# A recurrent attention cell followed by a gated feed-forward block: the first weight pieces asked for by ScalarE, first products in column halves, and a new order of the opening

## The chip, the cores and the metric

The kernel runs on one core of a Trainium2 chip. A core has TensorE (PE), VectorE (DVE), ScalarE (ACT), GpSimd (POOL) and SyncE (SP), and 16 DMA engines that serve the queues on which SP and ACT ask for transfers. The metric is the device time of one execution in microseconds. The time before is 514.01 us, the median of three runs (513.62 to 514.46).

## The reference

Two blocks follow each other. The first is a recurrent cell over 4 batches, 8 heads, 768 steps, 40 features per head; the second is a gated feed-forward block on the 3072 resulting rows of 320 features.

```
for t in range(S):
    m_new  = maximum(f[t] + m, i[t])
    C      = exp(f[t] + m - m_new) * C + exp(i[t] - m_new) * outer(v[t], k[t])
    n      = exp(f[t] + m - m_new) * n + exp(i[t] - m_new) * k[t]
    y[t]   = sigmoid(o[t]) * (C q[t]) / maximum(abs(n . q[t]), 1)
x   = y as rows of 8 heads x 40 = 320
out = (silu(x @ w_gate) * (x @ w_val)) @ w_out        # 320 -> 1536 -> 320
```

All inputs of the cell are float32. The three weight matrices arrive as float64, 3.9 MB each.

## The kernel before, in words

**Groups.** The 768 steps are cut into 6 groups of 128 steps for all 4 batches: 512 rows a group. For each group the cell is computed in closed form (scores of q and k, weighted with exponentials of the gates, times v, plus what the state of the steps before gives), and then the feed-forward block for these rows: 12 products of 128 hidden features each with gate and value weights (`hidden`, lines 698 to 712, the tile `gv_ps` in the profile), then `project_all` with the output weights. From the second group on, the function `gated` is used, and the cell of the next groups is woven in between.

**The opening.** Group 0 has a form of its own (functions named `first_...`). There the weights of all 128 by 128 pairs of steps stand in `W0`, 32 heads of 128 x 128, in the first 8 of 13 slices of `h_sb` (line 130). The order on TensorE, written out at lines 619 to 666, is: `burn` (products of a junk tile that nothing reads), the three products that build exponents (`first_mask`, `first_inputs`, `first_maxima`), for each half of the batches the transposes of k and q (`first_turn`), the scores (`first_scores`, whose results VectorE multiplies into `W0`, line 575), the products of `W0` with v (`first_own`, one call per batch u, 8 products of a 128 x 128 stationary tile with 41 columns), then on VectorE the division (`first_x`, lines 584 to 591) and the output gate (`first_gate`), the transposes of x into `xT` (`first_seam`), and the state for the groups behind (`first_state`, `first_kept`). Then the 12 products of `hidden` begin.

**Weights.** A float64 weight is loaded as two 32-bit words and turned into a float32 on the chip. The weights come in pieces (line 159): pieces 0 and 1 hold one slice of 128 hidden features each, pieces 2 to 6 two each, pieces 7 to 9 four slices of the output weights. `piece_load` (line 161) asks for a gate part of 5 chunks of 64 rows, and the value part as 4 chunks and 1 chunk, because the chunks of the value part are turned by one place. Before, the gate part is asked for on SP's queue and the two value parts on ACT's, for pieces 0 to 4. The raw words lie in a room of the pool `conv` (two rooms in turn) or in a tile that is free at the time (`home`: slices of `h_sb`, or `wo_sb`). The turn of one slice is `scale` (two ACT instructions into `top` and `low`, lines 212 and 214), `join` (two VectorE instructions, lines 221 and 222) and `rounded` (one addition, line 229, on POOL or VectorE).

**Order of the products.** `slots` (line 970) lists what is issued behind each of the 12 products, `ahead` which slices are converted in front of which. The gates of the steps behind the first 128 (`f_sb`, `i_sb`) are summed in `late_sums`, their running maximum is taken in `late_maxima`, goes through memory (`M_dram`) and comes back spread over partitions into `w_sb` (`weights_load`), from which the exponentials of group 1 are made (`weights_sub`, `weights_mask`, `weights_exp`).

**Queues.** Each engine works through its own instructions in order. SP's and ACT's transfers wait on 8 semaphores in turn, so a transfer is asked for only when the one eight before it has landed, and ACT does nothing else while one of its transfers waits to be asked for.

The lines around the change:

```
    nc.scalar.dma_start(out=f0, in_=spread_rows(f_gate))
    nc.sync.dma_start(out=i0, in_=spread_rows(i_gate))
    nc.scalar.dma_start(out=flat(f_sb), in_=gate_rows(f_gate)[:, L:])
    nc.scalar.dma_start(out=flat(i_sb), in_=gate_rows(i_gate)[:, L:])
    ...
    for P in range(2):
        load(k_sb, k, 0, P)
        load(q_sb, q, 0, P)
        load(v_sb, v, 0, P)
    load(o_sb, o_gate, 0, 0)
```

Of the kernel before, what the change touches and what calls it, by code (L numbers as in the profile page):

```python
# [18 lines left out]
L = 128  # L19
# [5 lines left out]
def kernel(  # L25
# [47 lines left out]
    def flat(t):  # L73
        return t.rearrange("p c t -> p (c t)")
# [79 lines left out]
    nc.scalar.dma_start(out=flat(f_sb), in_=gate_rows(f_gate)[:, L:])  # L154
    nc.scalar.dma_start(out=flat(i_sb), in_=gate_rows(i_gate)[:, L:])
# [5 lines left out]
    def piece_load(p, home=None):  # L161
        kind, m, n = PIECES[p]
        if kind == "gv":
# [4 lines left out]
            queues = (nc.sync,) + 2 * (nc.scalar if p < 5 else nc.sync,)  # L168
# [4 lines left out]
        if src[0][2].dtype == F32:  # L173
            for r, cs, w in src:
# [6 lines left out]
        if home is None:  # L181
            raw = conv.tile([128, 4 * NKC * 128], U32, name="raw")
        else:
            raw = home.rearrange("p a t -> p (a t)").bitcast(U32)
        raw = raw[:, 0:2 * a * d]
        for (r, cs, w), queue in zip(src, queues):
            queue.dma_start(out=raw[r].rearrange("p (a d) -> p a d", a=a)[:, cs], in_=w.bitcast(U32))
# [48 lines left out]
    for P in range(2):  # L236
        load(k_sb, k, 0, P)
        load(q_sb, q, 0, P)
        load(v_sb, v, 0, P)
# [339 lines left out]
    def first_own(u):  # L579
        first_y[u] = bank("first_y", "gen")[:, 0:H * D1].rearrange("p (h d) -> p h d", d=D1)  # L580
        for h in range(H):
            nc.tensor.matmul(first_y[u][:, h, :], lhsT=W0[:, u * H + h, :], rhs=v_sb[:, u * H + h, :], start=True, stop=True)  # L582
# [10 lines left out]
    def first_gate(P):  # L593
        for u in (2 * P, 2 * P + 1):
            x = x_sb[:, u, 0:DM].rearrange("p (h d) -> p h d", d=D)
            nc.vector.tensor_tensor(x, x, o_sb[:, u * H:(u + 1) * H], op=ALU.mult)
# [22 lines left out]
    burn(7)  # L619
# [8 lines left out]
    first_values(0)  # L628
    first_scores(0)
    first_own(0)  # L630
    late_sums()
    first_turn(1, k_sb, kT, (A, A))
    first_x(0)
    first_turn(1, q_sb, qT, (A, V))
    load(o_sb, o_gate, 0, 1)
    piece_load(0)
    first_own(1)
    first_values(1)
    first_scores(1)
    first_x(1)  # L640
    sig(0)
    piece_load(1)
    burn(3)
    first_own(2)
    piece_load(2, h_sb[:, 1:1 + NKC])
    sig(1)
    burn(2)
    first_own(3)
    first_gate(0)
    first_x(2)  # L650
    first_x(3)
    first_gate(1)
    first_seam(0, (A, A, V))
    scale(0)
    ps1 = first_state(1, "gen")
    burn(1, "gen")
    piece_load(3, h_sb[:, NH - NKC:])
    join(0)
    first_seam(1, (A, A, V))
    rounded(0, V)  # L660
    first_kept(0, first_state(0), A)
    first_kept(1, ps1, V)
    convert(1, V)
    nc.scalar.activation(warm, warm, AF.Silu)
    piece_load(4, wo_sb)
# [28 lines left out]

    def hid(g, m):
        return h_sb[:, m, :]
# [272 lines left out]
    ahead.update({4: [6], 5: [7, 8], 6: [9], 7: [10], 8: [11], 9: [], 10: [], 11: []})  # L969
# [138 lines left out]
```

## Time and profile before

| what | value |
|---|---|
| median of three runs | 514.01 us |
| the profiled execution, its own time | 513.3 us |
| its span, first to last instruction | 511.5 us |
| TensorE busy | 505.1 us, 99% |
| VectorE, ScalarE, GpSimd busy | 332.3, 204.8, 255.0 us |
| start of the first product of `hidden` | 31.92 us |
| start of `project_all` of group 0 | 95.03 us |
| DMA over the first 90 us | 17.57 MB, mean 195 GB/s |

In the views, a line of the timeline has the start in us, the duration or busy time in us, the engine, the line of the source, the operation, the tiles written and read, the shape and the number of instructions merged; in brackets the idle time of the engine before it and what ended it. Matrix products in float32 show as two records each. PEld is the loading of stationary tiles. A DMA view gives packets and bytes of each queue (q1 is SP's, q10 ACT's), with the time that the packets took as a share of 16 engines; the sums can pass 100%, as packets overlap.

### The profile page before, as it was taken

The numbers are of one execution on the slowest core, as the hardware profiler recorded it, in microseconds if no ns is written. First come the engines' busy times: TensorE is split into PE (matmuls) and PEld (weight loads), VectorE is DVE, ScalarE is ACT, GpSimd is POOL, SyncE is SP. The second block draws the span as 40 slices with busy tenths as digits, with TensorE's granted clock in tenths as the row PEclk, the third lists the DMA queues.
The fourth block names the chain that finished last, engine by engine and source line by source line (L and its number), as shares of the span: only waits on it lengthen the run. The fifth ranks groups of instructions, "written<-read, shape, count | busy, mean of one in ns | idle before, by whom it ended". The sixth has DMA issues, their size and how long they took to land.

```text
span 511.5 us, 14788 instructions
## 1 busy us (share of the span) xinstructions
PE 505.1 (99%) x6307; PEld 428.8 (84%) x6309; DVE 332.3 (65%) x539; ACT 204.8 (40%) x394; POOL 255.0 (50%) x274
## 2 busy tenths in 40 slices
PE   8999999999999999999999999999999999999997
PEld 4964445667888899988899888899988899988896
DVE  5779767887897777687466678467658554233421
ACT  3477655448512339312339321338421340223210
POOL 1303427475879663367652457652447650166710
PEclk9999999999999999999999999999999999999999
DMA  9999999698502992501993411993101200000001
GB/s 123 174 232 238 168 194 244 148 177 119 88 1 45 143 130 39 92 3 26 156 134 42 75 21 27 156 131 43 42 3 19 37 3 27 27 1 0 1 14 38
DMA packets 205497, 43.27 MB, mean 85 GB/s; under 512 B 193432, under 2 KB 200600, under 8 KB 205432
## 3 DMA queue, kind: packets, MB, share of 16 engines
q1 hardware_dynamic: 203444, 39.49, 49.4%
q10 hardware_dynamic: 1988, 2.85, 2.4%
q8 instruction: 49, 0.80, 0.7%
q14 instruction: 16, 0.13, 0.1%
HBM read 35.68 MB, written 4.01 MB: 78 GB/s over the span
## 4 chain that ended last, share of the span: by engine, by line
PE 91%; DMA 2%; DVE 2%; issue 1%; POOL 1%; ACT 1%; SPq 0%; DVEq 0%; ACTq 0%; POOLq 0%
PE gv_x L854 26%; PE o_ps L777 23%; PE gv_y L854 21%; PE gv_ps L706 5%; PE o_ps L723 5%; DMA w_sb<-M_dram 2%; PE inter L402 2%; PE intra L411 2%; PE sp L353 2%; PE first_y L582 1%; PE add L379 1%; POOL w_sb L493 1%; PE burn L521 1%; PE tp_kq L561 1%; PE sp L571 1%
## 5 line engine op out<-in xcount | busy, mean ns | idle before, releaser
L854 PE MATMUL gv_x<-xT,wgv_sb 64*128 64x256 f32 x720 | 89.1, 377 | 0.0
L854 PEld LDWEIGHTS gv_x<-xT,wgv_sb 64*128 64x128 f32 x720 | 69.6, 187 | 7.9 <-issue 0.2
L777 PE MATMUL o_ps<-wo_sb,h_sb 128*128 128x160 f32 x480 | 67.4, 300 | 0.0
L777 PEld LDWEIGHTS o_ps<-wo_sb,h_sb 128*128 128x128 f32 x480 | 65.6, 190 | 1.7 <-issue 1.7
L902 ACT ACTIVATE h_sb<-gv_x 128x256 f32<-128x256 f32 x30 | 11.5, 383 | 117.8 <-PE gv_x L854 117.8
L706 PE MATMUL gv_ps<-xT,wgv_sb 64*128 64x512 f32 x240 | 53.7, 596 | 0.3 <-DVE wgv_sb L229 0.3
L706 PEld LDWEIGHTS gv_ps<-xT,wgv_sb 64*128 64x128 f32 x240 | 23.6, 187 | 24.4 <-issue 23.2
L854 PE MATMUL gv_y<-q_sb,wgv_sb 64*128 64x256 f32 x360 | 44.0, 377 | 0.0
L854 PE MATMUL gv_y<-xT,wgv_sb 64*128 64x256 f32 x360 | 43.9, 376 | 0.0
L854 PEld LDWEIGHTS gv_y<-q_sb,wgv_sb 64*128 64x128 f32 x360 | 34.9, 187 | 4.2 <-DVE tmp L894 0.4
L854 PEld LDWEIGHTS gv_y<-xT,wgv_sb 64*128 64x128 f32 x360 | 35.0, 187 | 3.9
L364 POOL TENSOR_TENSOR vw_sb<-v_sb,w_sb 128x656 f32<-128x656 f32 x10 | 14.6, 1467 | 41.2 <-ACT w_sb L509 40.0
L777 PE MATMUL o_ps<-wT,S 128*128 128x160 f32 x240 | 33.4, 299 | 0.0
L777 PEld LDWEIGHTS o_ps<-wT,S 128*128 128x128 f32 x240 | 32.9, 190 | 0.0
L509 ACT ACTIVATE w_sb<-w_sb,g_T 128x64 f32<-128x64 f32 x128 | 31.0, 334 | 0.0
L854 PE MATMUL gv_x<-q_sb,sw 64*128 64x256 f32 x240 | 31.0, 376 | 0.0
L875 POOL TENSOR_TENSOR h_sb<-x_sb 128x512 f32<-128x512 f32 x12 | 15.8, 1314 | 24.6 <-ACT x_sb L874 24.6
L895 POOL TENSOR_TENSOR tmp<-tmp 128x512 f32<-128x512 f32 x15 | 20.0, 1332 | 14.5 <-DVE tmp L894 14.5
L875 POOL TENSOR_TENSOR h_sb<-tmp 128x512 f32<-128x512 f32 x13 | 16.5, 1269 | 21.5 <-ACT tmp L874 21.5
L744 POOL TENSOR_TENSOR S<-h_sb 128x256 f32<-128x256 f32 x30 | 22.6, 752 | 9.2 <-DVE h_sb L875 7.3
L854 PE MATMUL gv_y<-q_sb,sw 64*128 64x256 f32 x200 | 27.0, 388 | 0.0
L723 PE MATMUL o_ps<-wo_sb,h_sb 128*128 128x320 f32 x96 | 26.9, 437 | 0.0
(221 smaller groups left out, 984.6 us busy)
## 6 DMA issues: line engine op xcount, KB each, us to landing
w_sb<-M_dram SPq DMA_DIRECT2D x10, 512.0 KB, 7.1
k_sb<-in_k_dram SPq DMA_DIRECT2D x12, 320.0 KB, 7.4
v_sb<-in_v_dram SPq DMA_DIRECT2D x12, 320.0 KB, 5.5
o_sb<-in_o_gate_dram SPq DMA_DIRECT2D x12, 320.0 KB, 6.8
raw<-in_moe_w_out_dram SPq DMA_DIRECT2D x3, 1280.0 KB, 7.5
x_sq<-k_sb SPq DMA_DIRECT2D x64, 40.0 KB, 2.0
q_sb<-in_q_dram SPq DMA_DIRECT2D x32, 64.0 KB, 3.8
out_dram<-tmp SPq DMA_DIRECT2D x24, 80.0 KB, 1.7
```

Source lines behind the costliest of these rows:

```text
L353: nc.tensor.matmul(sp[two][half(i), a, :], lhsT=kT[feats(two), P * UA + a, half(i)], rhs=qT[feats(two), P * UA + a, half(i)], start=True, ...
L364: eng.tensor_tensor(vw_sb[:, heads(P)], v_sb[:, heads(P)], w_sb[:, heads(P), last].to_broadcast([128, UH, D1]), op=ALU.mult)
L402: nc.tensor.matmul(inter[two][half(i), a, :], lhsT=qT[feats(two), P * UA + a, half(i)], rhs=state(2 * n + i)[feats(two), P * UA + a, :], s ...
L509: nc.scalar.activation(w_sb[:, h], w_sb[:, h], AF.Exp, bias=g_T[:, n, h:h + 1], scale=-1.0)
L706: nc.tensor.matmul(ps[i], lhsT=wgv_sb[half(i), m, kc, :], rhs=x[half(i), kc, :], start=(kc == 0), stop=(kc == NKC - 1))
L723: nc.tensor.matmul(ps[u], lhsT=hid(g, m)[:, ts(u, L)], rhs=wo_sb[:, m, :], start=(m == 0), stop=(m == NFC - 1))
L744: eng.tensor_tensor(S1[:, k], lo[:, second_half], hi[:, second_half], op=ALU.add)
L777: nc.tensor.matmul(node[x][:, i], lhsT=lhs(k)[:, ts(i, L)], rhs=rhs(k), start=start and k == 0 and i == 0, stop=stop and k == KH - 1, skip ...
L854: nc.tensor.matmul(ps[:, i, cols], lhsT=lhs(c)[half(i)], rhs=rhs(c)[half(i)], start=start and c == 0, stop=stop and c == n - 1, skip_group ...
L875: (nc.vector if k == KH - 1 else nc.gpsimd).tensor_tensor(h_sb[:, 2 * k + 1], uw[:, 0], uw[:, 1], op=ALU.mult)
L895: nc.gpsimd.tensor_tensor(uw[:, :, second_half], uw[:, :, second_half], uw[:, :, first_half], op=ALU.add)
L902: nc.scalar.activation(h[:, first_half], x[:, 0, first_half], AF.Silu)
```

## The change

- ACT asks for pieces 0 and 1 in the beginning, in front of its first exponentials: gate part and first value part of each. The last value chunk (64 KB) goes to SP's queue, between the loads of k, q and v. Pieces 0 and 1 share one room of `conv`. For the other pieces the last value chunk moves from ACT's queue to SP's.
- The late gates (`f_sb`, `i_sb`) are asked for on SP behind piece 2, and `late_sums` moves from the opening to behind the first product of `hidden`; `late_maxima` and `late_decay` move to the place behind the second.
- `first_own` makes each product in two halves of 64 stationary columns.
- In the opening, `scale`, `join` and `rounded` of slice 0 move to between the transposes and scores of the second half; `rounded(0)` and `rounded(1)` go to POOL, and the first `first_gate` too. Both copies of the second q transposes are on ACT. `first_state(0)` goes in front of the seams. Of the `burn` products, burn(7) at the start becomes burn(5), and burn(3), burn(2), burn(1) between the later steps are gone.
- The rooms of raw pieces change: piece 2 in `conv`, piece 3 in slices 1 to 5 of `h_sb`. So the hidden features of the first group are written to other slices (`first_slots`).
- The load of `w_sb` goes in front of piece 6, the first steps on it one product earlier; the conversion of slices 10 and 11 one product later.

```diff
-    nc.scalar.dma_start(out=flat(f_sb), in_=gate_rows(f_gate)[:, L:])
-    nc.scalar.dma_start(out=flat(i_sb), in_=gate_rows(i_gate)[:, L:])
+    def late_gates():
+        nc.sync.dma_start(out=flat(f_sb), in_=gate_rows(f_gate)[:, L:])
+        nc.sync.dma_start(out=flat(i_sb), in_=gate_rows(i_gate)[:, L:])
...
+    raw_pair, homes = [], {}
+    def first_raw():
+        if not raw_pair:
+            raw_pair.append(conv.tile([128, 4 * NKC * 128], U32, name="raw"))
+        return raw_pair[0]
-    def piece_load(p, home=None):
+    def piece_load(p, home=None, parts=(0, 1, 2)):
...
-            queues = (nc.sync,) + 2 * (nc.scalar if p < 5 else nc.sync,)
+            queues = (nc.scalar if p < 2 else nc.sync, nc.scalar if p < 5 else nc.sync, nc.sync)
...
-        if home is None:
+        if p < 2:
+            raw = first_raw()[:, p * 2 * a * d:(p + 1) * 2 * a * d]
+        elif p in homes:
+            raw = homes[p]
+        elif home is None:
...
-    for P in range(2):
-        load(k_sb, k, 0, P)
-        load(q_sb, q, 0, P)
-        load(v_sb, v, 0, P)
+    load(k_sb, k, 0, 0)
+    load(q_sb, q, 0, 0)
+    piece_load(0, parts=(0, 1))
+    load(v_sb, v, 0, 0)
+    piece_load(1, parts=(0,))
+    load(k_sb, k, 0, 1)
+    piece_load(0, parts=(2,))
+    piece_load(1, parts=(1,))
+    load(q_sb, q, 0, 1)
+    load(v_sb, v, 0, 1)
+    piece_load(1, parts=(2,))
     load(o_sb, o_gate, 0, 0)
...
         for h in range(H):
-            nc.tensor.matmul(first_y[u][:, h, :], lhsT=W0[:, u * H + h, :], rhs=v_sb[:, u * H + h, :], start=True, stop=True)
+            for i in range(2):
+                nc.tensor.matmul(first_y[u][half(i), h, :], lhsT=W0[:, u * H + h, half(i)], rhs=v_sb[:, u * H + h, :],
+                                 start=True, stop=True)
...
-    def first_gate(P):
+    def first_gate(P, eng):
...
-            nc.vector.tensor_tensor(x, x, o_sb[:, u * H:(u + 1) * H], op=ALU.mult)
+            eng.tensor_tensor(x, x, o_sb[:, u * H:(u + 1) * H], op=ALU.mult)
...
-    burn(7)
+    burn(5)
...
     first_values(0)
+    load(o_sb, o_gate, 0, 1)
     first_scores(0)
     first_own(0)
-    late_sums()
     first_turn(1, k_sb, kT, (A, A))
     first_x(0)
-    first_turn(1, q_sb, qT, (A, V))
-    load(o_sb, o_gate, 0, 1)
-    piece_load(0)
     first_own(1)
+    scale(0)
+    first_turn(1, q_sb, qT, (A, A))
+    join(0)
     first_values(1)
+    first_x(1)
+    rounded(0)
     first_scores(1)
-    first_x(1)
+    piece_load(2, parts=(1,))
     sig(0)
-    piece_load(1)
-    burn(3)
+    piece_load(2, parts=(0, 2))
+    late_gates()
+    first_gate(0, G)
     first_own(2)
-    piece_load(2, h_sb[:, 1:1 + NKC])
+    piece_load(3, h_sb[:, 1:1 + NKC], (0, 2))
+    piece_load(4, wo_sb, (0, 2))
     sig(1)
-    burn(2)
     first_own(3)
-    first_gate(0)
     first_x(2)
+    ps0 = first_state(0)
     first_x(3)
-    first_gate(1)
+    first_gate(1, V)
     first_seam(0, (A, A, V))
-    scale(0)
+    first_kept(0, ps0, A)
+    first_seam(1, (A, A, V))
+    scale(1)
     ps1 = first_state(1, "gen")
-    burn(1, "gen")
-    piece_load(3, h_sb[:, NH - NKC:])
-    join(0)
-    first_seam(1, (A, A, V))
-    rounded(0, V)
-    first_kept(0, first_state(0), A)
+    join(1)
+    rounded(1)
+    piece_load(3, h_sb[:, 1:1 + NKC], (1,))
     first_kept(1, ps1, V)
-    convert(1, V)
+    convert(2, V)
+    piece_load(4, wo_sb, (1,))
     nc.scalar.activation(warm, warm, AF.Silu)
-    piece_load(4, wo_sb)
...
+    first_slots = (8, 9, 10, 11, 12, 0, 6, 7, 1, 2, 3, 4)
     def hid(g, m):
-        return h_sb[:, m, :]
+        return h_sb[:, first_slots[m], :]
...
-    ahead.update({4: [6], 5: [7, 8], 6: [9], 7: [10], 8: [11], 9: [], 10: [], 11: []})
+    ahead.update({4: [6], 5: [7, 8], 6: [9], 7: [], 8: [10], 9: [11], 10: [], 11: []})
     slots = {
-        0: [run(convert, 2, V), run(late_maxima), run(load_all, k_sb, k, 1),
-            run(nc.sync.dma_start, out=M_dram, in_=flat(M_sb)), run(load_all, q_sb, q, 1)],
-        1: [run(piece_load, 6), run(late_decay)],
-        2: [run(nc.scalar.activation, step1, step1, AF.Exp), run(decay_rows), run(weights_load, 1), run(load_all, v_sb, v, 1)],
+        0: [run(late_sums), run(load_all, k_sb, k, 1)],
+        1: [run(late_maxima), run(nc.sync.dma_start, out=M_dram, in_=flat(M_sb)), run(load_all, q_sb, q, 1),
+            run(weights_load, 1), run(piece_load, 6), run(late_decay)],
+        2: [run(nc.scalar.activation, step1, step1, AF.Exp), run(decay_rows), run(load_all, v_sb, v, 1)],
...
-        6: [run(turn, 1, (A, A), (A, V)), run(piece_load, 7)],
-        7: [run(weights_sub, 1, 0), run(weights_mask, 0), run(weights_sub, 1, 1), run(weights_mask, 1), run(nc.gpsimd.memset, q_sb, 0.0)],
-        8: [run(weights_exp, 0), run(weights_exp, 1), run(weigh_values, G, 0), run(weigh_values, G, 1),
-            run(piece_load, 8)],
+        6: [run(turn, 1, (A, A), (A, V)), run(piece_load, 7), run(weights_sub, 1, 0), run(weights_mask, 0), run(weights_sub, 1, 1), run(weights_mask, 1)],
+        7: [run(nc.gpsimd.memset, q_sb, 0.0), run(weights_exp, 0), run(weights_exp, 1), run(weigh_values, G, 0), run(weigh_values, G, 1)],
+        8: [run(piece_load, 8)],
```

## The prediction

> **What bounds the kernel now.** I read the page's engine shares, then the chain that ended last, then the timeline of the first 36 us and of 60 to 100 us, then the DMA queues in short windows.
>
> ```profile
> PE 505.1 (99%) x6307; PEld 428.8 (84%) x6309; DVE 332.3 (65%) x539; ACT 204.8 (40%) x394; POOL 255.0 (50%) x274
> PE 91%; DMA 2%; DVE 2%; issue 1%; POOL 1%; ACT 1%; SPq 0%; DVEq 0%; ACTq 0%; POOLq 0%
> ```
>
> TensorE is the bound and has work throughout. So the change can only move the time at which the dense products begin (31.92 us), and the stalls between there and the end of the first group.
>
> ```profile
> 1.19 3.17 PE L521 MATMUL burn<-junk 128*128 128x512 bf16 x7 [1.19 <-DVE warm L246]
> 11.24 1.08 PE L561 MATMUL tp_kq<-ident,q_sb 128*128 128x128 f32 x8
> 12.52 2.06 PE L571 MATMUL sp<-qT,kT 64*128 64x128 f32 x32 [0.20 <-ACT qT L142]
> 13.79 2.48 DVE L575 TENSOR_TENSOR h_sb<-sp,h_sb 128x512 f32<-128x512 f32 x4 [0.74 <-PE sp L571]
> 18.52 1.88 PE L582 MATMUL first_y<-v_sb,h_sb 128*128 128x41 f32 x16
> 20.32 2.06 PE L571 MATMUL sp<-qT,kT 64*128 64x128 f32 x32
> 28.04 1.13 PE L604 MATMUL add<-vw_sb,k_sb 128*64 128x41 f32 x32
> 29.33 1.25 PE L616 MATMUL tp_x<-ident,x_sb 128*128 128x128 f32 x10 [0.16 <-ACT top L212]
> 30.96 0.81 DVE L229 CUSTOM_DVE_ANT_0 wgv_sb<-wgv_sb,low 128x1280 uint16<-128x1280 uint16 x1
> 31.92 4.56 PE L706 MATMUL gv_ps<-xT,wgv_sb 64*128 64x512 f32 x20 [0.28 <-DVE wgv_sb L229]
> ```
>
> The opening is one chain: q lands, is turned (11.24), scores, VectorE's multiplications, own products, again for the second half (20.32), division, gate, seam (29.33). At its end the first dense product waits for VectorE's last step on slice 0 (30.96), 0.9 us after the first seam copies would have let it go.
>
> DMA windows at 18 to 19 us, at 19.5 to 21 us (as ACT's first piece comes in) and at 23.5 to 26 us:
>
> ```profile
> q1 hardware_dynamic: 1248, 0.20, 137.8%
> ...
> q10 hardware_dynamic: 245, 0.24, 58.5%
> q1 hardware_dynamic: 367, 0.06, 24.7%
> ...
> DMA packets 542, 0.52 MB, mean 209 GB/s; under 512 B 32, under 2 KB 542, under 8 KB 542
> ```
>
> Alone, SP's queue moves 0.20 MB in 1 us of small packets; beside the piece 0.06 MB in 1.5 us. The DMA engines have no room: a piece takes its time from the loads.
>
> **The change part by part.**
>
> *Pieces 0 and 1 early.* ACT asks for 320 + 256 + 320 + 256 = 1152 KB from about 2 us on, in front of nearly all of q, v and the second k; 160 KB of late gates leave that place. Net 992 KB (1.016 MB). Price per MB: in 19.5 to 21 us, 0.24 MB cost SP's queue 1.5 x 0.153 (153 GB/s over 10 to 19 us) - 0.06 = 0.17 MB, 1.1 us; for 1.016 MB 4.7 us. At 209 GB/s (23.5 to 26) it is 4.9 us. In 20 to 21 us, 0.22 MB took 75.4% of the engines' time, so 3.5 us. Over 4.5 to 8.5 us the queues moved only 137 GB/s where 198 were seen, room for 0.25 MB, so the low end is about 2 us, the high end 4.9. I take 4.3: the first row is nearest in kind, but its start-up lull is paid once in a burst. Landing times (issue plus time to landing): first q 2.26 + 8.7 = 10.96, now 15.3; second k 7.82 + 7.4 = 15.2, now 19.5; second q, turned at 17.6 and spaced like the others, 17.5, now 22.1 with the 64 KB chunk (0.3 us) ahead of it. o's second half was behind the pieces anyway and moves from 24.6 to about 27; its sigmoid is then done by 29, before the gate at 30. The Trainium skill, "DMA: Bandwidth & Descriptors", section "Issuing engines are not separate DMA queues", says that transfers asked for by several engines share the same 16 DMA engines and that only sequencer time is saved. By that rule the whole of 209 GB/s is paid, 4.9 us, and the sum below would be 0.6 us more, 515.5; the trace at 19.5 us leans that way.
>
> *The chain with these landings.* Turn of q 15.3, scores 1.28 later (as 11.24 to 12.52) 16.6; multiplications after 1.27, the first pair (1.24) done 19.1. An own product in halves has the form of line 604 (128 x 64 stationary, 41 columns, halves in turn): 1.13 us for 32 records against 1.88 now; I take 1.13, between -0.75 and 0. Four calls save 3.0 us of TensorE, of which two (1.5 us) are on the path. Own(0) until 20.2, turn of k 21.3, own(1) 22.5, turn of q (landed 22.1) 23.6. ACT copies k until 21.9, then scale(0) (0.81 + 0.70, as at 28.45) until 23.4, and only then the first q copy (0.6), 24.0: scale is queued ahead of the copy that the scores wait for. Scores 24.1, first pair of multiplications 26.6, all 27.85; own(2) beside, own(3) until 29.0; division (four steps, 1.1) 30.1, gate (0.88) 31.0, POOL's copy 0.35, seam with its first copies 1.35 (29.33 to about 30.5, one more copy in front): **first dense product at 32.7, 0.8 later than 31.92**. Without any delay of the loads the same chain would end at 28.4; break-even is a delay of 3.5 us. join(0) on VectorE (1.31, at 22.8) lies beside the turn of q; uncovered it costs 1.3. On POOL, rounded(0) (1.55, as at 43.22) stands ahead of the first gate (two of some 0.7, half of line 553's 1.29), done at 29.5; the seam needs it at 30.2. Late_sums leave VectorE (1.47) where it was not last. The burns gone were beside waits (they took 0.33 and 0.38 of the chain); two fewer at the start bring the exponents forward by at most 0.9, covered by the landing of q.
>
> *Dense products 0 to 5.* Slice 1 is now added on POOL: copies 0.55, scale 0.81, join 1.31, addition 1.55, some 0.1 between: 4.35 us after the first product starts, which takes 4.36. Slack zero, cost 0 to 1; take 0.2. Late_sums behind product 0 put a scan (1.47) in front of join(3), and a memset and a subtraction (0.62 + 1.53) in front of rounded(3) on POOL: it ends 13.0 after the start, where product 3 wants it at 13.1; cost 0 to 1; take 0.3. Behind these wait late_maxima, late_decay, join(4) and rounded(4); the transposes of the gates at 49.3 keep 1 us. On SP, the transfer of piece 3 waits for own(2), and with it pieces 4 and 5 and the second k loads; piece 3 is wanted after 42 and landed at 40.6 before. ACT's part of piece 3 is asked for only at 35 (28 before), 9 us to landing at most: 44 at worst, with the conversion due to begin by 43.
>
> *Later.* w_sb goes ahead of piece 6 (1280 KB, 6.4 us at 200 GB/s): landed at 72.7 before, now some 5 us earlier; piece 6 at 68.0 before, about 73, and slices 10 and 11 are converted one product (4.36) later, so covered. The exponentials come a product earlier. That removes this stall:
>
> ```profile
> 84.44 2.47 DVE L360 TENSOR_TENSOR w_sb<-sp,w_sb 128x512 f32<-128x512 f32 x4
> 85.78 2.33 PE L379 MATMUL add<-vw_sb,k_sb 64*64 64x41 f32 x126 [0.20 <-DVE w_sb L360]
> ```
>
> The products of line 379 wait for the banks that these multiplications free: 85.14 to 88.04 for what takes some 2.2 us. Gain 0 to 0.7; take 0.4. Piece 8 is asked for a product later and is wanted at 100, against 83 landed: no cost. The other slices of h_sb change addresses only.
>
> **Sum**: 0.8 + 0.2 + 0.3 - 0.4 = +0.9 us. The profiled execution took 513.3 (span 511.5 and 1.8 around), so 514.2; it stands 0.7 below the median of 514.01, against which the forecast is 514.9.
>
> **Rivals.**
>
> *A, faster: the loads lose little.* If the DMA engines fit the pieces into the room seen at 4.5 to 8.5 us, the delay is 2 us, and the start is 31.92 - 1.5; with +0.5 - 0.4 the time is 512.6. For it: that room; against it: SP's queue nearly stopping at 20 us. It decides below a delay of 2.4 us, where the sum passes -1.03.
>
> *B, slower: TensorE loses its pace.* With k landing at 12.8 and the exponent products over at 9.6, TensorE is idle for 3.2 us, then busy for 1.1, then idle again, without the burns. In the first 4 us of the trace seven burns take 0.45 each, though the granted clock reads full. If that pace came back until the products are dense again, scores(0) (2.06), own(0) (1.13 by the row) would take twice as long: +2.7 with some overlap, say +2.2, 517.1. The Trainium skill, "TensorE: Matmul & The Clock Gate", section "HAM oscillation — how this bites in real kernels", puts the limit at idle gaps of about 3.4 us. By that rule this gap is just too short; no gap so long is in this trace.
>
> *C, slower: the conversions become the bound.* POOL's additions at zero slack (0 to 1 each on slices 1, 3 and 4) or a late piece 3: +1.5 to 2 more, 516.6. For it: the weight loads of product 3 already waited 0.58 for POOL's addition before. Against it: VectorE's and ACT's waits there are short.
>
> *D, hidden anyway:* the delay equals what the chain gains, other parts cancel: 514.0.
>
> **How the numbers follow.** The bound for no change is 0.2%, 1.03 us, about what a measurement of this kernel can tell. Forecast 0.50 (own range 513.9 to 516.1: 0.25 within the bound, 0.22 slower, 0.03 faster); A 0.17, B 0.13, C 0.12 and D 0.08. Faster 0.20, same 0.33, slower 0.47. The range 512.8 to 517.1 leaves the far sides of A, B and C out.
>
> **What would show it.** In the profile after: packets of q10 in great number between 3.5 and 10 us with q1 low; first q's turn near 15 and the second scores near 24; own products at 1.13 a call; the first dense product at 32 to 33.5 and not waiting for VectorE's slice 0; line 379 without its wait. Wrong if q lands before 13 (A), if TensorE's records get longer between 10 and 25 us (B), or if dense products 1, 3 or 4 wait for POOL by more than 0.5 (C).

## The result, and the profile after

| kernel | median, us | range, us | runs |
|---|---|---|---|
| before, same chip | 514.09 | 512.08 to 515.30 | 6 |
| changed | 525.91 | 525.04 to 528.46 | 6 |

The ratio is 1.024, with an interval from 1.0211 to 1.0268: slower by 11.8 us, where 514.9 was forecast and 517.1 was the upper end. The profiled execution is the longest of the six (528.46; span 526.7, against 511.5 before), so its losses are some 2 to 3 us more than those of the others.

The page's engine shares and chain of the changed kernel:

```profile
PE 506.6 (96%) x6365; PEld 427.3 (81%) x6365; DVE 331.3 (63%) x534; ACT 204.7 (39%) x395; POOL 259.1 (49%) x278
PE 86%; DMA 5%; DVE 5%; SPq 2%; issue 1%; ACT 0%; POOL 0%; DVEq 0%; POOLq 0%
```

TensorE does the same work (506.6 against 505.1 us) in a longer span. DMA has 5% of the chain instead of 2%, VectorE 5% instead of 2%, SP's queue 2% instead of 0. So time went into waits, and the timeline says where. TensorE over the opening:

```profile
10.72 1.06 PE L582 MATMUL tp_kq<-ident,k_sb 128*128 128x128 f32 x8 [1.09 <-DMA k_sb<-in_k_dram]
17.16 1.94 PE L582 MATMUL tp_kq<-ident,q_sb 128*128 128x128 f32 x8 [5.38 <-DMA q_sb<-in_q_dram]
19.03 3.42 PE L592 MATMUL sp<-qT,kT 64*128 64x128 f32 x32
24.52 1.13 PE L604 MATMUL first_y<-v_sb,h_sb 128*64 128x41 f32 x32
...
33.63 2.69 PE L639 MATMUL tp_x<-ident,x_sb 128*128 128x128 f32 x20
36.25 0.90 PE L627 MATMUL add<-vw_sb,k_sb 128*64 128x41 f32 x24
38.62 0.43 PE L627 MATMUL add<-vw_sb,k_sb 128*64 128x41 f32 x8 [1.47 <-issue]
38.98 3.66 PE L733 MATMUL gv_ps<-xT,wgv_sb 64*128 64x512 f32 x8
```

q landed at 17.02 (10.96 before). Its turn took 1.94 instead of 1.08, the scores 3.42 instead of 2.06. The first dense product began at 38.98 instead of 31.92: 7.06 late.

Busy times in windows of 3.41 us of the same kernel (PE, PEld, DVE, ACT, POOL with instruction counts, then TensorE's granted clock, DMA share, GB/s):

```profile
11.67:15.09 3.42, 0.11 (x2) 0.00 (x0) 1.00 (x2) 0.00 (x0) 0.00 (x0) 1.00 1.34 148
15.09:18.50 3.41, 1.34 (x7) 1.38 (x8) 0.00 (x0) 0.22 (x1) 0.00 (x0) 0.50 1.21 153
18.50:21.91 3.41, 3.41 (x29) 3.08 (x29) 1.39 (x3) 2.34 (x5) 1.49 (x2) 0.50 1.17 138
...
28.74:32.15 3.41, 2.35 (x60) 1.92 (x57) 3.31 (x9) 1.65 (x3) 3.15 (x4) 1.00 1.00 221
...
35.56:38.98 3.42, 1.95 (x39) 1.62 (x39) 1.75 (x3) 2.63 (x6) 0.04 (x1) 1.00 1.06 200
38.98:42.39 3.41, 3.41 (x12) 1.53 (x10) 3.02 (x4) 2.85 (x4) 1.51 (x1) 0.50 1.06 216
```

The clock is 0.50 in the two windows behind the one in which TensorE waited for q, and again behind 35.56 to 38.98, where it was busy for 57%. Behind 28.74 to 32.15, busy for 69%, it stayed at 1.00.

Up to `project_all` the distance grew by 0.74 more (63.11 to 63.85 us): product 0 cost 1.7 at half pace, and the wait of line 379 that the prediction had shown went (the additions 2.08 against 2.84). Then comes a second large loss, in the exchange between the groups. SP's queue, VectorE and TensorE of the changed kernel:

```profile
75.06 13.52 SPq L201 DMA_DIRECT2D raw<-in_moe_w_out_dram  x2
88.67 6.33 SPq L138 DMA_DIRECT2D o_sb<-in_o_gate_dram  x2
127.62 10.60 SPq L358 DMA_DIRECT2D raw<-in_k_dram  x16
141.84 2.37 DVE L364 STREAM_TRANSPOSE kT<-raw 128x1024 f32<-128x1024 f32 x2 [6.80 <-DMA raw<-in_k_dram]
144.13 4.05 DVE L416 TENSOR_TENSOR C<-C,add 40x328 f32<-40x328 f32 x8
147.30 2.08 PE L881 MATMUL gv_x<-xT,wgv_sb 64*128 64x256 f32 x8 [4.99 <-DVE C L416]
```

and SP's queue and VectorE before:

```profile
72.06 2.46 SPq L187 DMA_DIRECT2D raw<-in_moe_w_out_dram  x2
74.57 8.11 SPq L138 DMA_DIRECT2D o_sb<-in_o_gate_dram  x2
116.89 9.26 SPq L337 DMA_DIRECT2D raw<-in_k_dram  x16
127.98 2.37 DVE L343 STREAM_TRANSPOSE kT<-raw 128x1024 f32<-128x1024 f32 x2 [3.54 <-DMA out_dram<-x_sb]
```

Pieces 7 and 8 are the two asks of the first line: before they were done in 2.5 us, now piece 8 waits on SP until 88.21, for the room that ScalarE's last step on slice 11 (87.38 to 88.19) frees; before it was asked for at 74.14. The gate o and all the transfers behind it wait in the same queue. The sixteen transfers of k come 10.7 later, VectorE turns them 13.9 later, the product `gv_x` waits 4.99 us for VectorE, and the clock falls again (0.50 from 144.79 to 151.62). From its start to its 40th and last record this product, the second of that name in the group, takes 11.5 us instead of 4.48 (139.56 to 151.08; 131.16 to 135.64 before): 7.0 lost.

So in the profiled execution 7.06 + 0.74, 0.34 in `project_all`, 0.25 in the additions to the state behind it and 7.0 in `gv_x` are 15.4 us; the span grew by 15.2.

### The profile page after: what moved, and what is told of

It is laid out like the page before. It is cut to its first block, busy times and chain, and to the rows that moved or that the text cites. A ratio compares the mean times of both kernels' runs of the same rounds, so it can differ in the third digit from the quotient of the medians.

```text
span 526.7 us, 14904 instructions
## 1 busy us (share of the span) xinstructions
PE 506.6 (96%) x6365; PEld 427.3 (81%) x6365; DVE 331.3 (63%) x534; ACT 204.7 (39%) x395; POOL 259.1 (49%) x278
## 4 chain that ended last, share of the span: by engine, by line
PE 86%; DMA 5%; DVE 5%; SPq 2%; issue 1%; ACT 0%; POOL 0%; DVEq 0%; POOLq 0%
PE gv_x L881 24%; PE o_ps L804 22%; PE gv_y L881 20%; PE gv_ps L733 10%; DMA q_sb<-in_q_dram 3%; PE sp L374 2%; PE inter L423 2%; PE intra L432 2%; DMA w_sb<-M_dram 2%; SPq L358 2%; PE add L400 1%; DMA raw<-in_k_dram 1%; DVE vw_sb L445 1%; PE sp L592 1%; DVE C L416 1%
## 5 line engine op out<-in xcount | busy, mean ns | idle before, releaser
L881 PE MATMUL gv_x<-xT,wgv_sb 64*128 64x256 f32 x720 | 90.3, 381 | 5.0 <-DVE C L416 5.0
L929 ACT ACTIVATE h_sb<-gv_x 128x256 f32<-128x256 f32 x30 | 11.5, 383 | 118.3 <-PE gv_x L881 118.2
L733 PE MATMUL gv_ps<-xT,wgv_sb 64*128 64x512 f32 x240 | 55.3, 611 | 0.0
```

Of the source, the lines that this page charges most:

```text
L733: nc.tensor.matmul(ps[i], lhsT=wgv_sb[half(i), m, kc, :], rhs=x[half(i), kc, :], start=(kc == 0), stop=(kc == NKC - 1))
L881: nc.tensor.matmul(ps[:, i, cols], lhsT=lhs(c)[half(i)], rhs=rhs(c)[half(i)], start=start and c == 0, stop=stop and c == n - 1, skip_group ...
L929: nc.scalar.activation(h[:, first_half], x[:, 0, first_half], AF.Silu)
```

## The experiments

"Before" and "after" in the diffs say which kernel was edited. Each ratio is to the kernel before, run beside it on the same chip. A run has 4 to 12 executions; the ratio is worked out from all of them and need not be the quotient of the medians. Executions of the kernel before itself lay between 511.49 and 518.23 us, so a difference of 1 us between two runs says little.

| run | edit | median, us | ratio (interval) |
|---|---|---|---|
| e1_order | after, slots 6 to 8 as before | 519.35 | 1.0135 (1.0096 to 1.0174) |
| e2_burn | after, burns while q is awaited | 522.29 | 1.0166 (1.0142 to 1.0189) |
| e3_early | before, pieces 0 and 1 early | 519.09 | 1.0109 (1.0086 to 1.0131) |
| e4_halves | before, halves | 514.72 | 1.0023 (1.0001 to 1.0045) |
| e5_order_burn | after, e1 and e2 together | 521.65 | 1.0138 (1.0096 to 1.0179) |
| e6_late | e1, pieces not early | 521.57 | 1.0124 (1.0088 to 1.0160) |
| e7_noburn | before, without the later burns | 518.74 | 1.0073 (1.0034 to 1.0113) |
| e8_piece0 | before, piece 0 alone early | 517.00 | 1.0055 (1.0022 to 1.0089) |
| e9_sig | before, sig(1) ahead of piece 2 | 516.75 | 1.0049 (1.0023 to 1.0076) |
| e10_halves_sig | e9 and halves | 519.01 | 1.0080 (1.0053 to 1.0107) |
| e11_noburn_sig | e9 without burns | 517.15 | 1.0050 (1.0028 to 1.0072) |
| e12_late_sig | e6, sig(1) first | 520.62 | 1.0111 (1.0083 to 1.0140) |
| e13_sp | before, values of pieces 2 to 4 on SP | 517.23 | 1.0095 (1.0062 to 1.0129) |
| e14_sp_halves | e13 and halves | 517.54 | 1.0086 (1.0056 to 1.0116) |
| e15_sp_noburn | e13 without burns | 517.28 | 1.0091 (1.0057 to 1.0125) |
| e16_late_sp | e12, values on SP | 524.22 | 1.0215 (1.0186 to 1.0244) |
| e17_halves_one_ask | before, halves, one ask on ScalarE | 516.18 | 1.0031 (1.0005 to 1.0057) |
| e18_halves_one_ask_noburn | e17 without burns | 515.72 | 1.0032 (1.0007 to 1.0058) |

None beats the kernel before; all but e16 lie within 2% of it.

**The late stall.** After, with slots 6 to 8 and the list of conversions as before, so that piece 8's room is free early:

```diff
-    ahead.update({... 6: [9], 7: [], 8: [10], 9: [11], ...})
+    ahead.update({... 6: [9], 7: [10], 8: [11], 9: [], ...})
-        6: [run(turn, ...), run(piece_load, 7), run(weights_sub, 1, 0), run(weights_mask, 0), ...],
+        6: [run(turn, ...), run(piece_load, 7)],
```

> The changed kernel with the order behind dense products 6 to 8 as it was before (slice 10 converted behind product 7, slice 11 behind 8, the steps on w_sb one product later, so that piece 8 is asked for earlier). Theory 1, the queue's order: in the changed kernel SP stands at piece 8 until 88.2 us (74.1 before), because its room is freed by the conversion of slice 11, and all loads behind it come late, the last of them the 16 of k that the state waits for (landed 141.6 against 127.8). Then piece 8 is asked for near 80, the products of the second group no longer wait 5 us for VectorE's additions to the state nor run at half pace behind that wait, and the time falls by 5 to 7 us, to 519 to 521. Rival, the late start alone: these loads are late only because everything began 7 us later; then the wait stays and the time stays within 1 us of 525.9.

Measured 519.35, 6.6 us less than the changed kernel (four executions from 517.49 to 522.99, the shortest profiled; by the ratios it is 5.4 us less). Piece 8 is asked for at 78.1, the sixteen transfers of k at 121.00, VectorE turns them at 132.18, and `gv_x` has no wait. SP's queue and TensorE of this run:

```profile
121.00 9.33 SPq L358 DMA_DIRECT2D raw<-in_k_dram  x16
...
131.48 1.13 PE L881 MATMUL gv_x<-xT,wgv_sb 64*128 64x256 f32 x8
132.44 1.03 PE L881 MATMUL gv_x<-q_sb,sw 64*128 64x256 f32 x8
```

It follows that the later conversions and piece 8 behind them are worth 5 to 7 us; the steps on w_sb went back by one product in the same edit.

**The clock while q is awaited.** After, with 24 burns between the turns of k and q:

```diff
     first_turn(0, k_sb, kT, (V, V))
+    burn(24)
     first_turn(0, q_sb, qT, (A, V))
```

> The changed kernel with 24 junk products between the transposes of the first k and the first q, where TensorE stands idle from 11.8 to 17.2 us. Theory, the pace: the granted clock is at half from 15.1 to 21.9 because TensorE had no work from 11.8 on; with the junk products it stays full, the transposes of q take 1.1 us (1.94 now), the scores 2.06 (3.42), the dense products begin 2 us earlier and the time falls by some 2 us, to 523.5 to 524.5. Rival, the loads alone set the opening: the time stays at 525.9 within 0.7, as what is gained is waited for at the second q.

Measured 522.29, 3.6 less than the changed kernel. TensorE of this run:

```profile
11.56 5.34 PE L542 MATMUL burn<-junk 128*128 128x512 bf16 x24
17.04 1.06 PE L582 MATMUL tp_kq<-ident,q_sb 128*128 128x128 f32 x8
18.34 2.06 PE L592 MATMUL sp<-qT,kT 64*128 64x128 f32 x32 [0.24 <-ACT qT L142]
```

q's turn and the scores are back at 1.06 and 2.06, the first dense product at 35.99, 3.0 earlier; the granted clock reads 1.00 up to the late stall, and half pace is left only there, from 140.29 to 143.70. The work in the wait is junk, so what it changed in the turn and the scores is the pace. The gap of 1.47 us in front of the first dense product is gone as well.

**Early asking by itself.** Before, with pieces 0 and 1 asked for by ScalarE in the beginning and the late gates on SP; and the same for piece 0 alone:

```diff
     load(q_sb, q, 0, 0)
+    piece_load(0, parts=(0, 1))
     load(v_sb, v, 0, 0)
+    piece_load(1, parts=(0,))          # not in e8
     load(k_sb, k, 0, 1)
...
```

> The kernel before with only the early asking: gate and first value parts of pieces 0 and 1 on ACT's queue in front of its exponentials, the last value chunks and the late gates on SP's queue behind the second k; everything else as before, the burns too. Theory, contention: the first q lands near 17 us (11.0 before) and the dense products begin 4 to 6 us later, with the pace at half in part of it; the time is 518 to 521. Rival, the other parts of the change made the loss in the opening (burns taken out, halves, POOL's additions): the dense products begin at 32 to 33 and the time stays within 1 us of 514.1.

> The kernel before with only piece 0 asked for early (576 KB on ACT's queue in place of the 1152 KB of both pieces), piece 1 at its old place, the late gates on SP's queue behind the second k. Theory, the DMA engines serve the piece in front of q, byte for byte: q lands near 13.5 (11.0 before, 15.9 with both pieces), the dense products begin 2.5 to 4 us after 31.9 and the time is 515.5 to 517. Rival, the burst costs the same whatever its size, or half pace makes most of the loss: 518.5 to 519.5.

Measured 519.09 and 517.00: 5.3 and 2.1 us over the medians of the kernel before beside them (513.76 and 514.86). With two pieces q landed at 15.90, with one at 13.92. TensorE of the first:

```profile
16.03 1.94 PE L575 MATMUL tp_kq<-ident,q_sb 128*128 128x128 f32 x8 [4.91 <-DMA q_sb<-in_q_dram]
17.90 3.79 PE L585 MATMUL sp<-qT,kT 64*128 64x128 f32 x32
...
38.80 6.71 PE L718 MATMUL gv_ps<-xT,wgv_sb 64*128 64x512 f32 x30 [0.28 <-DVE wgv_sb L235]
```

The first part of the change is harmful alone, roughly in proportion to its bytes, and by the two ways seen above: landing and clock. DMA queues from 8 to 12 us in the changed kernel, q10 being ScalarE's:

```profile
DMA packets 1370, 0.66 MB, mean 164 GB/s; under 512 B 857, under 2 KB 1370, under 8 KB 1370
q10 hardware_dynamic: 544, 0.53, 84.9%
q1 hardware_dynamic: 826, 0.13, 38.0%
```

Packets of the two queues come in like numbers (544 and 826), but ScalarE's carry 1 KB and SP's 160 B, so SP's queue got 0.13 of 0.66 MB. The Trainium skill, "DMA: Bandwidth & Descriptors", section "Queues, rings and completion order", says that each DMA engine takes the queues in turn, a packet at a time; the counts agree with it roughly, if the packets of this view are those of the page, which no run here shows.

**The two repairs together.** After, with e1 and e2.

> The changed kernel with both edits: the order behind dense products 6 to 8 as before, and 24 junk products while the first q is awaited. Theory, two separate causes: the gains add, 525.9 - 6.6 - 3.6 = 515.7, within 515 to 517.5, and what is left over the 513.8 of before is the late first q. Rival, the gains overlap (both take away half-pace behind the late wait in the second group): 518 to 519.5.

Measured 521.65: no gain over e1 alone (519.35; by the ratios the two are alike), and neither of the two times expected. ScalarE of this run:

```profile
27.25 0.74 ACT L536 ACTIVATE o_sb<-o_sb 128x640 f32<-128x640 f32 x1
33.88 0.74 ACT L536 ACTIVATE o_sb<-o_sb 128x640 f32<-128x640 f32 x1 [5.89 <-DMA o_sb<-in_o_gate_dram]
```

The second half of o, asked for at 23.83, landed at 33.85; ScalarE had asked for 512 KB of piece 2 at 25.25, only 1.42 us behind it. Over four kernels the time to landing falls with that distance: 1.42 us apart 10.0 us, 1.50 (e2) 7.9, 2.45 (e1) 5.8, 2.78 (the changed kernel) 5.9. It looks as if what the loads of q had suffered now befell o; no run changes the distance alone, so this is argued, not shown. What the trace does show is that the second gate, the transposes and the first dense product (39.14) waited for o.

**The parts that are left.** Before, with halves alone; without the burns; and the changed kernel with e1 and with pieces 0 and 1 at the places of before:

```diff
-    burn(7)                            # e7; e4 has only the halves of the change
+    burn(5)
...
-    burn(3)
...
-    burn(2)
...
-    burn(1, "gen")
```

> The kernel before with only the first own products in halves of 64 columns. Theory: a call takes 1.13 us in place of 1.88, as in the changed kernel; the last two calls are on the path in front of the division, so the dense products begin 0.5 to 1.2 us earlier, and the time is 512.9 to 513.6. Rival: the calls wait for VectorE's multiplications and the last steps are VectorE's conversion of slice 0, so the time stays at 514.1 within 0.3.

> The kernel before with the burns taken out as in the change: five at the start in place of seven, none later. Theory: what let the pace fall is the idle time that the late q makes; in the kernel before TensorE has work enough without the six later burns (they fill 1.8 us of 31), so the pace stays full and the time is within 0.7 us of 513.8. Rival, the burns hold the pace: half pace in one window of 3.4 us or two in the opening, 515.5 to 517.5.

> The changed kernel with the order behind products 6 to 8 as before, and with pieces 0 and 1 asked for, and slice 0 converted, at the places of the kernel before; halves, the missing burns, the gate on POOL, the late gates, the rooms and the place of w_sb's load stay changed. Theory: the early asking is what made the opening long; the first q lands at 11 again, the dense products begin at 31 to 33 and the time is 512.5 to 515. Rival: the other parts cost by themselves (missing burns and half pace, POOL's additions late for product 1 or 3): 516 or more.

Measured 514.72, 518.74, 521.57. At first sight the second says that the burns keep the pace, and the third that something else in the change costs 7 us. The traces say otherwise: in all three the second sigmoid of o (sig(1)) comes late, at 27.73, 29.54 and 32.64 instead of 26.80, behind ScalarE's asks for pieces. An ask waits for the transfer eight places back, counted over both queues; which one that is moves with each edit (piece 0's gate part at 26.17 before, piece 1's or 2's at 28.9 and 31.1 in e7 and e6). Four runs put sig(1) ahead of the asks for piece 2:

```diff
-    piece_load(2, h_sb[:, 1:1 + NKC])
     sig(1)
+    piece_load(2, h_sb[:, 1:1 + NKC])
```

> Kernel before, with one swap: the sigmoid of the second output gate (sig(1)) is issued on ScalarE ahead of ScalarE's asks for piece 2 instead of behind them. Theory R (ScalarE's asks wait for the transfer eight places back, and the sigmoid waits behind them): sig(1) moves from 26.80 us to about 24.7, when the second half of o lands. In the kernel before VectorE reaches the second gate only at 28.08, so nothing on the path moves: 514.1 +- 0.5, first dense product at 31.9. Theory P (piece 2 asked for later, by the 0.7 us of the sigmoid, holds up the conversions): slower by 0.5 to 1.

> Kernel before with products of first values in 64-column halves, and sig(1) ahead of ScalarE's asks for piece 2. Halves alone gave 514.7 and a second gate that waited for sig(1) at 27.73. Theory R: without the wait behind the asks the second gate follows own(3) (24.9), seam 1 starts near 27.1 against 29.33, and slice 0 (piece landed 26.2 to 27.1, 3.3 us from its first step to the last) is ready at 29.5 to 30.4: first dense product near 30.4, time 512.6. Rival H (halving is worth nothing by itself, the path is somewhere else): 514 or more, first dense product at 31.5 or later.

> Kernel before with burn(7) as burn(5), without burn(3), burn(2), burn(1), and sig(1) ahead of ScalarE's asks for piece 2. Without the swap the same kernel took 518.7, its sig(1) came at 29.54, and TensorE idled 2.13 us and then ran at half pace. Theory R: the loss was the ask on ScalarE, which waited for a transfer that landed at 28.9; with the swap sig(1) is at 24.7, no idle time, no half pace: 514.2 +- 0.6. Rival W (the burns themselves keep TensorE at full pace): half pace somewhere between 25 and 40 us, 516.5 or more.

> The changed kernel with the order of slots 6 to 8 as before, pieces 0 and 1 asked for and slice 0 converted at the places of before, and sig(1) ahead of the asks for piece 2. Left of the change: halves, no burns in between, first gate on POOL, late gates on SP, the rooms, w_sb ahead of piece 6. Without the swap it took 521.6, its own products done at 23.55 and sig(1) at 32.64. Theory R: sig(1) at 24.7, seam 1 near 26, slice 0 ready 29 to 30, first dense product near 30, 512.5 (512 to 513.5). Rival M (one of the parts left costs by itself: the gate on POOL, the rooms, or the late gates): first dense product after 32, or a stall behind it, 515 or more.

All four missed (516.75, 519.01, 517.15, 520.62): the wait was not removed but moved, in e9, e10 and e11 to the copies of the transposes. ScalarE of e9_sig (ACTq are its asks):

```profile
24.77 0.74 ACT L515 ACTIVATE o_sb<-o_sb 128x640 f32<-128x640 f32 x1 [2.85 <-DMA o_sb<-in_o_gate_dram]
24.86 5.09 ACTq L187 DMA_DIRECT2D h_sb<-in_moe_w_val_dram  x2
29.99 0.59 ACT L142 COPY xT<-tp_x 128x512 f32<-128x512 f32 x1 [4.48 <-PE tp_x L616]
```

and of e10_halves_sig:

```profile
24.96 6.40 ACTq L187 DMA_DIRECT2D h_sb<-in_moe_w_val_dram  x2
31.41 0.58 ACT L142 COPY xT<-tp_x 128x512 f32<-128x512 f32 x1 [5.80 <-DMA raw<-in_moe_w_gate_dram]
```

The sigmoid is early, as expected, and the two asks behind it now hold ScalarE for 5 to 6 us. In e12 it waited in piece 1's ask until 31.11. What the rivals had named was seen, half pace without burns in e11 (33.50 to 36.91) and a first dense product at 37.90 in e12, but behind these waits, so neither rival is settled by it. So the next runs took the asks away from ScalarE:

```diff
-            queues = (nc.sync,) + 2 * (nc.scalar if p < 5 else nc.sync,)
+            queues = (nc.sync,) + 2 * (nc.scalar if p < 2 else nc.sync,)
```

> Kernel before, with the value parts of pieces 2 to 4 asked for by SyncE instead of ScalarE, so that ScalarE asks for nothing between piece 1 and the first dense product. Theory R (ScalarE's wait for the transfer eight places back holds up what stands behind it): in the kernel before this wait is short (ask at 24.67, done 26.76) and the second gate follows VectorE (28.08), so 514.2 +- 0.5, first dense product at 31.9. Theory P (these asks are late on SyncE and the conversions of slices 2 to 5 wait): a stall of PE before 50 us, slower by 1 to 3.

> The same, with products of first values in 64-column halves. Theory R: nothing holds the seam up any more; own products end at 24.9, seam 1 near 27.2, slice 0 ready 29.5 to 30.4, first dense product near 30.4: 512.7. Rival H (halves are worth nothing): first dense product at 31.5 or later, 514 or more.

> The same as the first (value parts of pieces 2 to 4 on SyncE), with burn(7) as burn(5) and without burn(3), burn(2), burn(1). Theory R: the 518.7 and 517.2 of the two kernels without burns came from ScalarE's asks; now 514.2 +- 0.6 and full pace throughout. Rival W (the burns keep the pace): half pace between 20 and 40 us and 516.5 or more.

> The changed kernel with the order of slots 6 to 8 as before, pieces 0 and 1 asked for and slice 0 converted at the places of before, sig(1) ahead of piece 2, and all value parts behind piece 0 asked for by SyncE. Theory R: sig(1) near 24.7, no idle time of 5 us in the transposes of x, first dense product near 30: 512.5 to 513.5. Rival M (the gate on POOL, the rooms or the late gates cost by themselves): 515 or more with a wait that names them.

Measured 517.23, 517.54, 517.28, 524.22. The head did what was expected: first dense product at 32.10 in e13, at 30.79 with halves. But the loads of q for group 1 were late. TensorE of e13_sp:

```profile
59.58 0.66 PE L318 MATMUL tp_kq<-ident,k_sb 64*128 64x64 f32 x16
62.33 0.77 PE L318 MATMUL tp_kq<-ident,q_sb 64*128 64x64 f32 x16 [2.09 <-DMA q_sb<-in_q_dram]
62.85 3.65 PE L706 MATMUL gv_ps<-xT,wgv_sb 64*128 64x512 f32 x8
```

The wait takes 2.09, and the products behind it run at half pace. This is the price that the expectation gave to its theory P, at another load. Without burns (e15) half pace came at 25.86, behind a stretch of own products only, and the first dense product at 34.51 instead of 32.10, as the rival W has it. The median is still that of e13, because the late start and the late q cover each other (e15 has no wait for q), so this pair cannot tell what the burns are worth. In e16 ScalarE stood in piece 0's asks until 26.5, so it told nothing of the parts.

The last two keep both queues and leave ScalarE one ask, which waits for o:

```diff
-            queues = (nc.sync,) + 2 * (nc.scalar if p < 5 else nc.sync,)
+            queues = (nc.sync, nc.scalar if p < 5 else nc.sync, nc.scalar if p < 5 and p != 2 else nc.sync)
...
-    piece_load(3, h_sb[:, NH - NKC:])
+    piece_load(3, h_sb[:, NH - NKC:], (0,))
...
     rounded(0, V)
+    piece_load(3, parts=(1, 2))
```

> Kernel before with 64-column halves; the last value chunk of piece 2 asked for by SyncE, and ScalarE's two asks for piece 3 moved behind slice 0's last step. So the only ask ahead of sig(1) waits for o's second half, which sig(1) needs anyway. Theory R (the halves' gain was lost at ScalarE's asks): sig(1) at 24.7 to 25.4, first dense product near 30.8, k loads of group 1 as before (landed by 57, wanted at 58.5), 513.0 (512.5 to 513.5). Rival H: 514 or more, first dense product at 31.5 or later, or half pace in the opening all the same.

> The same, with burn(7) as burn(5) and without burn(3), burn(2), burn(1). The waits of ScalarE and SyncE are nearly the same in both. Theory R (burns lay beside waits): 513.0 +- 0.5, no half pace. Rival W (burns hold the pace through the stretch of own products): half pace somewhere in 20 to 32 us, first dense product at 32 or later, 515 or more.

Measured 516.18 and 515.72, both at full pace in their profiles. The first dense product began at 31.12 and 30.93, near what was expected, but the time did not follow. ScalarE and TensorE of e17:

```profile
31.12 8.85 PE L714 MATMUL gv_ps<-xT,wgv_sb 64*128 64x512 f32 x40 [0.71 <-DVE wgv_sb L234]
38.01 0.79 ACT L217 ACTIVATE top<-h_sb 128x640 f32<-128x640 f32 x1
41.20 9.21 PE L714 MATMUL gv_ps<-xT,wgv_sb 64*128 64x512 f32 x40 [1.23 <-DVE wgv_sb L234]
...
136.25 1.13 PE L862 MATMUL gv_x<-xT,wgv_sb 64*128 64x256 f32 x8 [1.67 <-DVE C L400]
```

and TensorE of e18 in the second group:

```profile
135.25 1.14 PE L859 MATMUL gv_x<-xT,wgv_sb 64*128 64x256 f32 x8 [1.20 <-DVE C L400]
```

Product 2 waits 1.23 us for slice 2: piece 2 landed at 37.45, and ScalarE began on it at 38.01 (36.98 before). Until 35 us the kernel before had moved 5.85 MB, e13 5.76, e14 5.83, e17 5.76: whatever the head did, the bytes came no earlier. So what was won at the head (0.8 and 1.0 us) is gone at product 2, which begins at 41.20 in e17 and 40.49 in e18, and at 40.58 before. The rest is lost in the second group, where `gv_x` waits again for the state, 1.67 and 1.20 us: e18 reached `project_all` at 94.95, like the kernel before (95.03), and ended 1.8 us behind it. The last transfer of k landed at 130.56 and 129.57 instead of 127.76; why, no run shows. That the halves are worth nothing (rival H) is right in the sum, though its sign, a late first dense product, was not seen. And the burns between the steps are worth nothing here, where the pace stays full without them: 515.72 without, 516.18 with.

## Why the prediction was wrong

- *What bounds the kernel*: right. TensorE does the same work, and only the start of the dense products and the stalls up to the end of the first group changed.
- *q's delay, "I take 4.3", between 2 and 4.9*: the mechanism was right (e3), the size not: 6.1 in the profiled execution, and 4.9, 5.4 and 5.9 in e1, e5 and e2, where everything asked for up to there is the same (q landed at 15.84, 16.32 and 16.90). So the range ended where the measurements begin. The high end took 209 GB/s from 23.5 to 26 us. Beside q the DMA engines moved 176 GB/s (4 to 6 us) and 164 (8 to 12), by which the net 1.016 MB is 5.8 to 6.2 us. The room read from 137 GB/s over 4.5 to 8.5 us was not there: with the pieces the queues moved 165 GB/s in that stretch, not the 198 of a later one. Nor does a low end of 2 us follow from room for 0.25 MB; the 0.77 MB left are 3.7 us at 209 GB/s. Rival A, that the loads lose little, falls with the same numbers; the 4.9 us that the prediction worked out by the rule of the Trainium skill came nearer than the forecast.
- *The clock, rival B, 0.13, +2.2*: it came, with its condition (TensorE idle for q). The idle gap was put at 3.2 us, with k landing at 12.8 and q at 15.3; k was turned at 10.72 and q at 17.16, and the gap was 5.38. Its price in the head is 0.86 on the turn and 1.36 on the scores, 2.2 as forecast, but two more places fell to half pace, the first dense product (1.7) and the exchange (about 2.1 of the 7.0). e2 puts all that it takes away up to and in the first dense product at 3.6. The prediction held the rival unlikely because the Trainium skill, "TensorE: Matmul & The Clock Gate", section "HAM oscillation — how this bites in real kernels", sets the limit at an idle gap of 3.4 us. The gap of 5.38 passes that limit, so here the size of the gap was wrong and not the rule. At the first dense product no gap was longer than 1.47 us, and there the runs show another limit: a share of a window.
- *The end of the chain, "seam with its first copies 1.35", then the first dense product at 32.7*: a term is missing. Between the last transposes of x (done at 36.3) and the first dense product (38.98) stand the 32 products of the second state (line 627): 1.1 us, and the gap of 1.47 us in the midst of them. Of the 6.3 us by which the head missed 32.7, these are 2.6, the clock 2.2 and q's landing 1.8, a little more than the whole.
- *Halves, 1.13 a call*: right (1.13). That the saving is worth 1.5 on the path was wrong: with halves the first dense product began at 32.73 in e4, 30.79 in e14 and 31.12 in e17 (31.92 before), and none of the three ended sooner. What they bring forward waited for the second sigmoid of o in e4, for q of group 1 in e14, and for slice 2 and the state in e17.
- *"The burns gone were beside waits"*: held in e17 against e18, both at full pace. e7 seemed to refute it, but there ScalarE's asks were late; in e15 half pace came without such a wait. Whether the burns are needed for the pace in a kernel without halves stays open.
- *Conversions, +0.2 and +0.3, and rival C*: not seen. Beyond product 0 at half pace the dense stage lost nothing.
- *Line 379, -0.4*: -0.76. The wait went, as forecast.
- *"Piece 8 is asked for a product later and is wanted at 100, against 83 landed: no cost"*: this step failed most. The landing of piece 8 itself was looked at, not the queue behind its ask, where o, q and k for the next groups stand. It was asked for 14 us later (74.14 to 88.21). Of these 7 are the late start of the dense products; the other 7, where one product is 4.36, come from its room, which hangs on slice 11. Worth 6.6 us by e1's median.

So the sum put two terms at nothing, the late stall (6.6 by e1) and the clock (3.6 by e2, the gap with it), and q's landing 1.8 too low. Added these are 12.0, where 10.9 are missing (11.8 less 0.9); how far they overlap e5 cannot tell, since there the late o took part of the gain. Two things stay open: what the gate on POOL, the rooms and the late gates cost by themselves, since ScalarE's asks came in between in each run made for it (in e6 and e12 the first transposes of x wait 0.87 and 1.24 us for POOL's gate, but the late sigmoid comes behind it); and the gap of 1.47 us at 37.15 in the changed kernel. In e1 the additions stop for 2.44 us at the same instruction (24 records done of 32). In both a 16 KB transfer of instructions had ended 1.5 and 1.6 us before the additions went on; with 24 burns more in the stream (e2) there is no gap. That it is the loading of code is only argued.

## What to carry to other kernels

Where an ask is moved, ask what its room waits for and list everything behind it in its queue up to the next exchange; the transfer's own due time says little. Where an engine both computes and asks for transfers, any edit can change which transfer its next ask waits for, so read that engine's asks in the trace before a gain or a loss is put down to the edit. And a gain at the head of a stage counts only if the next inputs come earlier too: here the weights came no earlier, and a later exchange took what was left.

## What was not expected of the hardware

*The clock goes by windows of 3.41 us and by TensorE's busy share in them.* Over the changed kernel and the sixteen experiments in which the clock fell, windows at full pace with TensorE busy for up to 57% were followed by half pace in thirty cases and by full pace in three (43% in e11 at 135.9 us, 51% in e13 and 56% in e12 near the end); windows with 58% or more by full pace, but for e15 (busy by the trace for 95%, nearly all of it own products of 41 columns). Out of half pace, windows of up to 83% busy were followed by half pace again, and of the 25 windows with 86% or more all but five by full pace; the five (e4, e6, e7, e12, e15) hold the additions or own products of 41 columns. But so do two that came back (e15 at 29.28, e16 at 33.60), so that records of few columns count for less than their time is a guess. Idle gaps of 0.87 (e12) and 1.42 us (e6) were enough where the share was 44 or 45%. The Trainium skill, "TensorE: Matmul & The Clock Gate", section "What's actually happening", gives about 3.4 us for an idle and for a busy window; the length agrees, but no window here had to be idle as a whole.

*The same DMA engines moved more in some stretches in which both queues had work.* From 35 to 45 us they moved 278 GB/s in the kernel before, where both queues had work, and 212 in e13, where SP's queue had all of it. e14, e15 and e16, with next to nothing on ScalarE's queue there, moved 208 to 209, and e18, with both, 274; but e17 and the changed kernel, also with both, 232 and 212. DMA of the kernel before in this stretch:

```profile
DMA packets 1456, 2.78 MB, mean 278 GB/s; under 512 B 97, under 2 KB 97, under 8 KB 1456
q1 hardware_dynamic: 885, 1.75, 68.4%
q10 hardware_dynamic: 571, 1.04, 36.9%
```

and of e13_sp:

```profile
DMA packets 1099, 2.12 MB, mean 212 GB/s; under 512 B 65, under 2 KB 65, under 8 KB 1099
q1 hardware_dynamic: 1099, 2.12, 106.4%
```

The packets took like shares of the engines' time (105% and 106%), so the queue in e13 did not run empty; a packet took longer. But two queues are not enough: from 25 to 35 us the two kernels moved 2.19 and 2.14 MB, and from 32 to 34 us the kernel before moved 214 GB/s with 120 and 113 packets on its two queues. The condition stays open. The Trainium skill, "DMA: Bandwidth & Descriptors", section "Issuing engines are not separate DMA queues", says that asking from several engines saves only their time to ask. From 35 to 45 us the difference is not time to ask; what else makes it is not shown.
